# Masked attention and expert layers on one core: the last pattern matmul goes into the next head pair, transposes and maxima stand in twos, and the finishing work is spread

## The chip, the cores and the metric

The kernel runs on one core of a Trainium2 chip. The metric is the device time of the core in microseconds. Before the change it is 882.85 us, the median of three runs (878.72 to 883.02).

A core has engines that run side by side and each take their own instructions in order: PE (TensorE, matmuls and transposes), DVE (VectorE), ACT (ScalarE), POOL (GpSimd) and SP, which here mostly issues transfers (DMAs).

## The reference

Four batches with eight heads of 768 positions and 64 dimensions go through attention that lets a query see only the keys of its own hash bucket; the result, 3072 rows of 512, goes through a router and eight experts.

```python
q_bits = (einsum('bhsd,dk->bhsk', q, proj) > 0)      # 6 bits; the same for k
mask = q_bucket[:, :, :, None] == k_bucket[:, :, None, :]
scores = where(mask, (q @ k.T) / 8, -1e9)
attn = exp(scores - scores.max(-1)); attn /= attn.sum(-1) + 1e-9
x = (attn @ v).transpose(0, 2, 1, 3).reshape(3072, 512)
logits = x @ w_gate + modality_bias[modality_id]     # 8 experts
e = argmax(logits); gate = softmax(logits)[e]
out = gate * (relu(x @ w1[e]) @ w2[e])               # 512 -> 1024 -> 512
```

## The kernel before

**Two halves.** Up to some 540 us the core works on attention, in 16 steps, one for each pair of heads (`i` = 0 to 15, four to a batch). Behind that stands the expert phase, which multiplies blocks of 256 gathered rows (slots) with the weights of one expert, while the weights stream in as blocks of 512 KB (tile `raw`), are cast by ACT (L749) and split into a high and a low part by DVE or POOL (L751).

**A step and its letters.** In attention the scheduler orders every engine but PE; PE's order is written by hand. A step goes through six key tiles (`kt` = 0 to 5), and for each of them the table `PLAN` (L30 to L37) has a string. Each letter lets one generator go on by one piece:

- `S`, scores (L305, L306): one block of 128 keys by 512 queries for each head and then one for the last 256 queries of both. ACT exponentiates each (L318, L323), POOL adds the exponentials up (L326, tile `sp`).
- `A`, weighting (L341): the exponentials times the values, two key tiles later. `Q` (L359): column sums of the step before. `v`, `V` (L286): sums of the values.
- `M`, the maxima for the next step, i+1 (L239; L245 for two blocks of 256 at once). Each block goes into one of two buffers `psm`, from which DVE takes a maximum (L241, L247).
- `B`, late: the maxima, turned with a transpose into one of the buffers `psx` (L268), go into the operands on DVE (L270, L271).
- `W`, `T`, for steps i+3 and i+2: `W` splits the inputs (L162 on ACT, L166 on DVE and POOL). There are twelve `T`: six groups of four transposes (L180), copied out by ACT (L184), two sign blocks (L207; DVE, L209), and four pattern matmuls (L222): half 0 for both heads, then half 1 for both. Each pattern matmul fills a buffer `psx`, which L223 copies (ACT for half 0, DVE for half 1) and L224, a relu on ACT, reads too.

The buffers `psx` are two, shared by `T`, `B`, `V`, `Q` and the finishing; `psm` are two, the scores' `pss` two.

**Finishing.** When a batch's four steps are done, `finish` brings its sums into shape, takes reciprocals and routes its rows to experts (L374 to L413 and what they call), and `finish_x` turns six tiles of rows (L422), scales them on DVE (L424, tile `xs`, two buffers) and writes them to the memory tensor `x_d` (L426, on SP's queue). For batches 0 to 2 the letters `F`, `f` and `x` place this in steps 4 to 6, 8 to 10 and 12 to 14; for the last batch it runs among the first experts' work.

**The end.** Most slots are always done. Whether a few more are needed is known only on the chip: the tile `tot` holds two counts, and `conditional` (L904 on) makes two chains of branches from them, each of which loads its count into a register of every engine (L908, L910). With these inputs both chains are left at their first branch.

## Time and profile before

| quantity | value |
|---|---|
| median of three runs | 882.85 us |
| the profiled execution: its own time; span from first to last instruction | 881.03 us; 879.3 us |
| busy: PE, DVE, ACT, POOL | 814.8, 589.3, 502.9, 457.8 us |
| matmuls on PE | 5154 |
| granted TensorE clock, mean | 0.983 |
| step ends: sums matmuls L359 in the chain of waits | 81.00, 111.21, 141.47, 171.71 us |

The page has the busy time of each engine and its idle time by what ended it. The waits are a list for one engine: line and tile that waited, the engine and line that released it, and then the total, the number and the longest. Windows give busy times in stretches of the span. In the timeline a row is start, duration, engine, line, operation, tiles and shapes, and in brackets the idle time before it with its releaser; matmuls overlap, so from one to the next it is the starts that count, not the durations.

### The profile page before, as it was taken

What the parts mean: (1) busy time and instruction counts of PE and PEld (TensorE: products, weight loads), DVE (VectorE), ACT (ScalarE), POOL (GpSimd) and SP (SyncE); (2) the same over time, 40 slices, a digit from 0 to 9 for tenths busy, and PEclk for the clock granted to TensorE, in tenths of its full rate; (3) what the DMA queues carried; (4) which work ended last, traced back from release to release, by engine and by line L of the source; (5) the groups of instructions that cost most, each with busy time, mean ns of one, the idle gap of its engine ahead of it and who ended that gap; (6) DMA issues with size and microseconds to landing.
All of it is one profiled execution on the core that took longest, in us unless ns stands there. A gap on an engine that the chain in (4) does not pass through costs nothing.

```text
span 879.3 us, 14545 instructions
## 1 busy us (share of the span) xinstructions
PE 814.8 (93%) x5154; PEld 581.1 (66%) x5154; DVE 589.3 (67%) x1029; ACT 502.9 (57%) x949; POOL 457.8 (52%) x347
## 2 busy tenths in 40 slices
PE   6799999989899989899989998989999999999991
PEld 3555556555555555555555554879999999998981
DVE  6776766687676597676697685965656565657650
ACT  4466756656656656656655464455555555557550
POOL 5376687667877658868657697421222221212110
PEclk9699999999999999999999999999999999999996
DMA  6422213213323212322201432797777777679630
GB/s 170 109 73 73 66 43 91 63 28 91 88 75 91 73 28 81 88 82 66 54 18 38 143 110 81 198 251 243 223 222 234 221 213 227 218 225 300 204 129 14
DMA packets 76757, 110.92 MB, mean 126 GB/s; under 512 B 10495, under 2 KB 52095, under 8 KB 76672
## 3 DMA queue, kind: packets, MB, share of 16 engines
q1 hardware_dynamic: 71744, 96.72, 38.3%
q0 software_dynamic: 4928, 13.14, 4.0%
q8 instruction: 45, 0.74, 0.4%
q14 instruction: 40, 0.33, 0.1%
HBM read 84.83 MB, written 13.33 MB: 112 GB/s over the span
## 4 chain that ended last, share of the span: by engine, by line
PE 74%; DVE 12%; ACT 4%; DMA 3%; issue 3%; POOL 2%; SPq 0%; POOLq 0%; DVEq 0%; ACTq 0%
PE psu L341 13%; PE pss L305 8%; PE pss L306 6%; PE psm L239 5%; PE hps L786 5%; PE hps L788 4%; PE hps L787 4%; PE yps L830 4%; PE yps L828 4%; PE yps L829 4%; PE psx L180 3%; PE psx L207 2%; PE psm L245 2%; DVE mx L241 2%; DVE w L751 2%
## 5 line engine op out<-in xcount | busy, mean ns | idle before, releaser
L326 POOL TENSOR_TENSOR sp<-sp,pb 128x768 f32<-128x768 f32 x124 | 228.5, 1865 | 43.1 <-ACT pb L323 41.6
L751 DVE TENSOR_TENSOR w<-raw,w 128x1024 fp32r<-128x1024 f32 x108 | 136.7, 1268 | 90.6 <-ACT w L749 88.7
L749 ACT CAST w<-raw 128x1024 fp32r<-128x1024 f32 x112 | 117.0, 1047 | 61.5 <-PE yps L830 51.5
L241 DVE TENSOR_REDUCE mx<-psm 128x1 f32<-128x512 f32 x192 | 128.5, 686 | 26.3 <-PE psm L239 24.9
L341 PE MATMUL psu<-pb,vt 128*64 128x512 f32 (+1 forms) x768 | 144.8, 498 | 0.0
L318 ACT ACTIVATE pb<-pss 128x512 f32<-128x512 f32 x192 | 114.9, 599 | 48.8 <-PE pss L306 38.0
L323 ACT ACTIVATE pb<-pss 128x512 f32<-128x512 f32 x96 | 57.5, 599 | 132.8 <-PE pss L306 131.1
L786 PE MATMUL hps<-xh,w 128*128 128x256 f32 x384 | 108.9, 284 | 3.7 <-DVE hl L793 3.6
L787 PE MATMUL hps<-xl,w 128*128 128x256 f32 x384 | 108.9, 284 | 0.0
L788 PE MATMUL hps<-xh,w 128*128 128x256 f32 x384 | 108.5, 283 | 0.0
L341 PEld LDWEIGHTS psu<-pb,vt 128*64 128x64 f32 x768 | 46.7, 136 | 87.4 <-issue 87.2
L763 POOL DMA_INDIRECT xg<-x_d,tb x26 | 30.9, 1190 | 126.6 <-DMA tb<-tab 88.7
L836 POOL DMA_INDIRECT out<-y,tb x26 | 32.7, 1257 | 109.7 <-ACT y L835 56.2
L828 PE MATMUL yps<-w,hl 128*128 128x512 f32 x208 | 82.8, 398 | 0.8 <-DVE hl L816 0.8
L830 PE MATMUL yps<-w,hh 128*128 128x512 f32 x208 | 81.4, 391 | 0.0
L247 DVE TENSOR_REDUCE mx<-psm 128x2 f32<-128x512 f32 x96 | 66.1, 688 | 22.8 <-PE psm L245 17.8
L829 PE MATMUL yps<-w,hh 128*128 128x512 f32 x208 | 81.2, 390 | 0.0
L305 PE MATMUL pss<-m_0g,s_0g 128*128 128x512 f32 x192 | 77.9, 406 | 0.0
L166 POOL TENSOR_TENSOR n<-qk,n 128x384 fp32r<-128x384 f32 x36 | 40.5, 1130 | 70.9 <-ACT n L162 60.7
L786 PEld LDWEIGHTS hps<-xh,w 128*128 128x128 f32 x384 | 73.4, 192 | 5.1 <-DVE hl L793 4.3
L787 PEld LDWEIGHTS hps<-xl,w 128*128 128x128 f32 x384 | 73.6, 192 | 1.7 <-issue 1.2
L788 PEld LDWEIGHTS hps<-xh,w 128*128 128x128 f32 x384 | 73.5, 192 | 0.0
(210 smaller groups left out, 1766.7 us busy)
## 6 DMA issues: line engine op xcount, KB each, us to landing
raw<-moe_w SPq DMA_DIRECT2D x112, 512.0 KB
qk<-q SPq DMA_DIRECT2D x32, 192.0 KB
qk<-k SPq DMA_DIRECT2D x32, 192.0 KB
vt<-v SPq DMA_DIRECT2D x16, 384.0 KB
x_d<-xs SPq DMA_DIRECT2D x24, 256.0 KB
m_1g<-m_1g SPq DMA_DIRECT2D x16, 192.0 KB
s_1g<-s_1g SPq DMA_DIRECT2D x16, 192.0 KB
m_0g<-m_0g SPq DMA_DIRECT2D x15, 192.0 KB
```

The lines of the kernel that those rows point to most:

```text
L241: nc.vector.tensor_reduce(out=mx[:, qt + j, hi, 0:1], in_=mp, axis=AX.X, op=ALU.max)
L305: nc.tensor.matmul(out, t["s1"][h][:, ks], t["m1"][h][:, cs], start=True, stop=False)
L326: (nc.vector if h and i in CFG["spd"] else nc.gpsimd).tensor_tensor(out=t["sp"][:, h], in0=(t["pb"][0] if kt == 1 else t["sp"])[:, h], in1 ...
L341: nc.tensor.matmul(t["u"][part][64 * h:64 * h + 64, 0:w], t["v"][:, h, kt], t["pb"][kt][:, h, COLS[part]], start=False, stop=(kt == NT - 1 ...
L749: nc.scalar.copy(out=hi, in_=r)
L751: (nc.gpsimd if pool else nc.vector).tensor_tensor(out=lo, in0=r, in1=hi.bitcast(F32), op=ALU.subtract)
L786: nc.tensor.matmul(hps, lo[:, c, fs], xh[:, c], start=(c == 0), stop=False)
L787: nc.tensor.matmul(hps, hi[:, c, fs], xl[:, c], start=False, stop=False)
L788: nc.tensor.matmul(hps, hi[:, c, fs], xh[:, c], start=False, stop=(c == 3))
L828: nc.tensor.matmul(yps[g], hl[fc][:, gs], hi[:, fb], start=(fc == 0), stop=False)
L829: nc.tensor.matmul(yps[g], hh[fc][:, gs], lo[:, fb], start=False, stop=False)
L830: nc.tensor.matmul(yps[g], hh[fc][:, gs], hi[:, fb], start=False, stop=(fc == 7))
```

## The change

There are five parts in one edit.

1. The table. The last of a step's twelve `T`, the pattern matmul of head 1, half 1, gets a letter of its own, `P`, and is done in the next step behind its first score block. The groups of transposes stand two by two (`TT` in kt 0, 1 and 2), and so do most maxima (`MM`).
2. The finishing pieces have other places: new letters `e` and `E` let `finish` go on in the third and fourth step of a batch, and the six tiles of rows go into two steps, three each (`x` and `y`), instead of one.
3. In steps 0 and 1 two of the pattern copies (L223) each go from DVE to ACT; later steps are as before.
4. The last batch's six writes of rows are issued on ACT's queue instead of SP's.
5. `tot` has a third entry, worked out on DVE, that says whether any further slot is needed, and one branch on it stands around both chains.

```diff
 PLAN = (
-    "LvSMTMSASfMTMfx",
-    "SMTVMSASfMTMfx",
-    "SMTMSAQFlSMTMfx",
-    "SMSATFWSBfMx",
-    "SFWMSATSMfTFMWx",
-    "SMFTSATSTFWBx",
+    "LvSPMMTTSASfMMfexy",
+    "SMMTTSASfMVMey",
+    "SMMTTSAQFlSMMEfxy",
+    "SMSATWSBMEe",
+    "SWMSATFSMTMfWExe",
+    "SMTSATSBFfFfWe",
 )
...
-                (nc.vector.tensor_copy if half or i == 0 else nc.scalar.copy)(out=t["m1"][h][PT[h], hs], in_=pp[0:64, 0:HALF])
+                (nc.vector.tensor_copy if (half if i > 1 else i + h == 0) else nc.scalar.copy)(out=t["m1"][h][PT[h], hs], in_=pp[0:64, 0:HALF])
...
-            nc.sync.dma_start(out=xv[:, tt], in_=xs)
+            (nc.scalar if b == B - 1 else nc.sync).dma_start(out=xv[:, tt], in_=xs)
...
-            ts = chain(turn(i + 2), signs(i + 2), patterns(i + 2)) if i + 2 < NPR else iter(())
+            last, ts = ts, chain(turn(i + 2), signs(i + 2), patterns(i + 2)) if i + 2 < NPR else iter(())
...
+                    elif c == "P":
+                        next(last, None)
...
-                    elif c == "x":
-                        if i % 4 == 2:
-                            if kt == 0 and i > 4:
-                                xs = finish_x(i // 4 - 1, 0, NT)
-                            next(xs, None)
-                            next(xs, None)
-                            next(fins, None)
+                    elif c == "e" and i % 4 >= 2 or c == "E" and i == NPR - 2:
+                        next(fins, None)
+                    elif c == "x" and i % 4 == 2 or c == "y" and i % 4 == 3:
+                        if c == "x" and kt == 0 and i > 4:
+                            xs = finish_x(i // 4 - 1, 0, NT)
+                        next(xs, None)
+                        next(xs, None)
...
-        tot = const.tile([P, 2], I32, name="tot")
+        tot = const.tile([P, 3], I32, name="tot")
...
+        nc.vector.tensor_scalar(out=over[:, 0:1], in0=cu[:, E - 1:E], scalar1=SURE_BIG + 0.5, scalar2=None, op0=ALU.is_gt)
+        nc.vector.tensor_scalar(out=over[:, 1:2], in0=su[:, E - 1:E], scalar1=SURE_SML + 0.5, scalar2=None, op0=ALU.is_gt)
+        nc.vector.tensor_tensor(out=over[:, 0:1], in0=over[:, 0:1], in1=over[:, 1:2], op=ALU.max)
+        nc.vector.tensor_copy(out=tot[:, 2:3], in_=over[:, 0:1])
...
-        rest("b", SURE_BIG, NBIG, 0)
-        rest("s", SURE_SML, NSML, 1)
+        more = nc.values_load(tot[0:1, 2:3], min_val=0, max_val=1, skip_runtime_bounds_check_because="0 or 1")
+        with tc.If(more > 0):
+            rest("b", SURE_BIG, NBIG, 0)
+            rest("s", SURE_SML, NSML, 1)
```

On PE, where one ordinary step ends and the next begins (the numbers at names are buffers; L222 is a pattern matmul with its weight load, L268 `B`, L180 the transposes). Before:

```order
L222 MATMUL psx<-bits_172,pat 128x384
L305 MATMUL pss<-m_0g_111,s_0g_113 128x256
L306 MATMUL pss<-m_0g_115,s_0g_117 128x256
L305 MATMUL pss<-m_1g_112,s_1g_114 128x256
L306 MATMUL pss<-m_1g_116,s_1g_118 128x256
L222 LDWEIGHTS pat
L222 MATMUL psx<-bits_172,pat 128x384
L268 MATMUL psx<-identr,nm_1417 128x128 x2
L305 MATMUL pss<-m_0g_122,s_0g_124 128x512
L306 MATMUL pss<-m_0g_126,s_0g_128 128x512
L239 MATMUL psm<-s_0g_102,m_0g_100 128x512
L180 MATMUL psx<-identr,n_1340 128x128 x4
```

And at the same place with the change:

```order
L222 MATMUL psx<-bits_172,pat 128x384
L305 MATMUL pss<-m_0g_111,s_0g_113 128x256
L306 MATMUL pss<-m_0g_115,s_0g_117 128x256
L305 MATMUL pss<-m_1g_112,s_1g_114 128x256
L306 MATMUL pss<-m_1g_116,s_1g_118 128x256
L268 MATMUL psx<-identr,nm_1417 128x128 x2
L305 MATMUL pss<-m_0g_122,s_0g_124 128x512
L306 MATMUL pss<-m_0g_126,s_0g_128 128x512
L222 LDWEIGHTS pat
L222 MATMUL psx<-bits_172,pat 128x384
L239 MATMUL psm<-s_0g_102,m_0g_100 128x512 x2
L180 MATMUL psx<-identr,n_1340 128x128 x8
```

Between the last two pattern matmuls now stand `B` and a score block, the maxima are two at once, and the transposes eight at once.

Further on in the same step, from the end of kt 0 into kt 1, PE has with the change:

```order
L245 MATMUL psm<-s_0g_102,m_0g_100 128x256 x2
L239 MATMUL psm<-s_1g_103,m_1g_101 128x512
L305 MATMUL pss<-m_0g_122,s_0g_124 128x512
L306 MATMUL pss<-m_0g_126,s_0g_128 128x512
L239 MATMUL psm<-s_1g_103,m_1g_101 128x512
L245 MATMUL psm<-s_1g_103,m_1g_101 128x256 x2
L180 MATMUL psx<-identr,n_1340 128x128 x4
```

Before, four transposes stood between L245 and the first L239 and behind the second; now four blocks of maxima go by with one score block among them.

On DVE, from kt 2 into kt 3 of an ordinary step (L166 splits an input for step i+3, L364 adds the column sums, L255 joins maxima), the pieces stood before:

```order
L241 TENSOR_REDUCE mx_1157<-psm 128x1
L364 TENSOR_TENSOR gs<-gs,psx 128x384
L241 TENSOR_REDUCE mx_1157<-psm 128x1
L247 TENSOR_REDUCE mx_1157<-psm 128x2
L241 TENSOR_REDUCE mx_1157<-psm 128x1
L255 TENSOR_REDUCE m_1315<-mx_1157 128x8
L166 TENSOR_TENSOR n_1404<-qk,n_1404 128x6x64
```

With the change:

```order
L241 TENSOR_REDUCE mx_1157<-psm 128x1
L166 TENSOR_TENSOR n_1404<-qk,n_1404 128x6x64
L364 TENSOR_TENSOR gs<-gs,psx 128x384
L241 TENSOR_REDUCE mx_1157<-psm 128x1
L247 TENSOR_REDUCE mx_1157<-psm 128x2
L241 TENSOR_REDUCE mx_1157<-psm 128x1
L255 TENSOR_REDUCE m_1315<-mx_1157 128x8
```

The split L166 has come ahead of three maxima.

## Prediction

> **What bounds the kernel now.** The page comes first: PE is busy 93% of the span, no other engine above 67%, and three quarters of the chain that ended last is PE's.

> ```profile
> PE 814.8 (93%) x5154; PEld 581.1 (66%) x5154; DVE 589.3 (67%) x1029; ACT 502.9 (57%) x949; POOL 457.8 (52%) x347
> PE 74%; DVE 12%; ACT 4%; DMA 3%; issue 3%; POOL 2%; SPq 0%; POOLq 0%; DVEq 0%; ACTq 0%
> ```

> So time is to be won where PE stands still, and the list of PE's waits says for what (total, times, longest):

> ```profile
> PE psx L268 <- ACT s_0g L224: 16.1, 14, 2.0
> PE psm L239 <- DVE mx L247: 5.2, 6, 1.4
> PE hps L786 <- DVE hl L793: 3.6, 2, 3.0
> ```

> The largest comes once a step: `B` waits for a relu. The windows, one step each, show what a batch's finishing adds (columns: stretch, length, PE busy):

> ```profile
> 141.50:171.70 30.20, 29.12 (x186) 17.24 (x189) 19.91 (x35) 19.98 (x42) 22.22 (x16) 1.00 0.24 65
> 171.70:205.00 33.30, 31.09 (x202) 18.46 (x203) 28.68 (x59) 20.32 (x43) 21.70 (x16) 1.00 0.20 53
> 205.00:239.20 34.20, 31.78 (x214) 19.04 (x214) 23.97 (x43) 19.99 (x43) 29.34 (x23) 1.00 0.29 74
> 239.20:271.50 32.30, 31.07 (x202) 19.06 (x206) 23.25 (x39) 19.97 (x42) 22.08 (x16) 1.00 0.33 101
> ```

> The first is an ordinary step: PE idles 1.08. Finishing adds 1.97 + 2.66 + 1.95 = 6.6 of PE work, and idle time beyond 1.08 of 1.13 + 1.34 + .15 = 2.6.

> **The step's end**, a gain. The timeline of an ordinary step:

> ```profile
> 156.00 0.34 PE L222 MATMUL psx<-bits,pat 128*128 128x384 bf16 x1
> 156.04 0.41 PE L305 MATMUL pss<-m_0g,s_0g 128*128 128x256 f32 x1
> 156.30 0.28 PE L306 MATMUL pss<-m_0g,s_0g 128*128 128x256 f32 x1
> 156.41 0.28 PE L305 MATMUL pss<-m_1g,s_1g 128*128 128x256 f32 x1
> 156.65 0.34 PE L222 MATMUL psx<-bits,pat 128*128 128x384 bf16 x1
> 156.91 0.60 ACT L323 ACTIVATE pb<-pss 128x512 f32<-128x512 f32 x1 [0.34 <-PE pss L306]
> 157.53 0.49 ACT L224 ACTIVATE s_0g<-psx 64x384 fp32r<-64x384 f32 x1
> 158.07 0.36 PE L268 MATMUL psx<-identr,nm 128*128 128x128 f32 x2 [1.08 <-ACT s_0g L224]
> 158.27 0.47 PE L305 MATMUL pss<-m_0g,s_0g 128*128 128x512 f32 x1
> 158.58 0.40 PE L306 MATMUL pss<-m_0g,s_0g 128*128 128x512 f32 x1
> 158.81 0.40 PE L239 MATMUL psm<-s_0g,m_0g 128*128 128x512 f32 x1
> 159.05 0.46 PE L180 MATMUL psx<-identr,n 128*128 128x128 f32 x4
> 159.34 0.47 PE L239 MATMUL psm<-s_0g,m_0g 128*128 128x512 f32 x1
> ```

> The two pattern matmuls of 156.00 and 156.65 fill both `psx`; `B` needs one, and the first comes free when the relu at 157.53 is done. A pattern matmul holds PE's issue .04 (156.00 to 156.04), so PE stands from 156.69 to 158.07: 1.38. With the change `B` finds the buffer of an earlier pattern free and goes at 156.65, taking .20 (158.07 to 158.27), the score block .54 (to 158.81). `P` could go at 157.39 but needs the buffer of 156.00, free as before at 158.07, the exponential and relu ahead being the same: .68 remains. `P`'s own relu then stands behind the next exponential (.60 + .49), and the second of `TT`, which takes `P`'s buffer, waits for it; two maxima (.24 each, 158.81 to 159.05) and a transpose block (.29) cover all but .19. And what follows a pattern matmul comes late: 156.04 to 156.30 is .26, 156.30 to 156.41 .11; behind `B` that lay in the stall, behind `P` it costs .14. Together 1.38 − .68 − .19 − .14 = **.37 gained**.

> A matmul behind a transpose block takes .47 (159.34) instead of .40 (158.81): three blocks fewer stand alone, .2 gained.

> **The maxima**, a loss. How near may they stand?

> ```profile
> 152.31 0.39 PE L239 MATMUL psm<-s_1g,m_1g 128*128 128x512 f32 x1
> 152.74 1.29 DVE L241 TENSOR_REDUCE mx<-psm 128x1 f32<-128x512 f32 x2 [0.31 <-PE psm L239]
> 153.48 0.50 PE L245 MATMUL psm<-s_1g,m_1g 128*128 128x256 f32 x2
> 143.59 0.40 PE L305 MATMUL pss<-m_0g,s_0g 128*128 128x512 f32 x1
> 144.06 0.39 PE L239 MATMUL psm<-s_0g,m_0g 128*128 128x512 f32 x1
> ```

> With two `psm`, a third block must wait for the first one's reduction: at the earliest 1.17 behind the first block (152.31 to 153.48); a fourth for the second's, which ends at 154.03, 1.72 behind the first block and with a release of .04 1.76. A score block takes .47 (143.59 to 144.06). From kt 0 to kt 1 the changed order has two blocks, a score block, two blocks: the third comes at .24 + .24 + .47 = .95 and waits .22; the fourth would come at 1.41 and waits .35. From kt 1 to 2 a `V` stands between the first two; the third is then in time, the fourth waits about .3. From kt 2 to 3 three blocks in the first pattern: .22. Together **1.1 lost** a step. Less, if pieces of finishing stand there; more, if DVE brings its reductions late: L166 now stands ahead of three of them.

> ```profile
> L166 DVE TENSOR_TENSOR n<-qk,n 128x384 fp32r<-128x384 f32 x28 | 25.3, 905 | 15.5 <-issue 13.8 <-POOL sp L326 1.3
> ```

> By its mean of .9, where a score block and the sums give DVE room, I count nothing and .2 as the upper bound.

> So an ordinary step changes by −.37 − .2 + 1.1 = +.53, times 14: **+7.4**. Bounds: half of the maxima's waits covered, 14 × 0 = 0; .2 more each, +10.

> **Finishing.** Of the idle 2.6 a batch the spreading can take all, or (bound above) leave it and add as much again, since reciprocals and row scalings come on DVE ahead of reductions that PE now waits for. The pieces still are chains PE to DVE to PE, and I take 2.0 of idle time, counting in that `x` and `y` fill some waits of the maxima: −.6 for each of two batches. For the third, whose steps 14 and 15 are next, +.4. Sum **−.8**, from −8 to +8.

> **Steps 14 and 15.**

> ```profile
> 491.09 0.50 PE L239 MATMUL psm<-s_1g,m_1g 128*128 128x512 f32 x1 [1.39 <-DVE mx L247]
> 540.55 0.85 PE L359 MATMUL psx<-sp,ones 128*32 128x384 f32 x8 [0.68 <-POOL sp L326]
> ```

> The wait of 1.39 is for a reduction that DVE runs late in the crowded step 14; with three row tiles fewer it goes: −1.4. Three row tiles move to step 15, where PE waits for other engines anyway; −.7, as at 540.55. Against that, the rows land later, and in POOL's order a gather that needs them now stands ahead of three of the last step's `sp` additions, for which 540.55 waits: taken at +1.2, between 0 and two such additions, which the page has at 1.9 each (next fence). Sum **−.9**.

> ```profile
> L326 POOL TENSOR_TENSOR sp<-sp,pb 128x768 f32<-128x768 f32 x124 | 228.5, 1865 | 43.1 <-ACT pb L323 41.6
> ```

> **The last batch's rows.** In the chain and the timeline:

> ```profile
> 569.57 8.66 DMA x_d<-xs
> 578.33 1.29 DVE L424 TENSOR_TENSOR xs<-psx,rin 128x512 f32<-128x512 f32 x2 [5.18 <-DMA x_d<-xs]
> 579.53 3.48 DVE L751 TENSOR_TENSOR w<-raw,w 128x1024 fp32r<-128x1024 f32 x3
> 583.41 0.39 PE L786 MATMUL hps<-xh,w 128*128 128x256 f32 x1 [3.00 <-DVE hl L793]
> 853.21 2.90 DMA out<-y,tb
> 568.30 0.20 DVE L705 CAST tot<-lcu 128x1 int32<-128x1 f32 x1
> ```

> A row write, issued on SP's queue among the weight loads, takes 8.66; with both `xs` taken, DVE waits 5.18, its splits come late and PE loses 3.00. The nearest transfer on another queue, the output's, takes 2.90. By that DVE's wait falls away, and with it PE's: **−3.0**. ACT now stands at those issues until DVE has scaled the rows, its casts behind; bounds −3.0 and +1. The four operations for `tot` lie ahead of the same wait of DVE's and cost nothing; without that cover four times the .2 of the cast at 568.30, .8.

> [...]

> **One branch instead of two.**

> ```profile
> L908 POOLq TENSOR_LOAD <-tot x2: 306/404/503, 862.4 to 869.2; - x2
> L910 POOLq INC_SWDGE_SEM  x2: 1677/1692/1708, 867.5 to 870.4; - x2
> L970 POOLq DRAIN  x3: 40/107/6286, 872.1 to 879.0; - x3
> ```

> POOL ends the program: it loads the second count at 869.2, adds to its semaphore at 870.4 for 1.7, and then drains from 872.1 for 6.3. One chain fewer takes 872.1 − 869.2: **−2.9**. Bounds: 0, should the drain wait for the last output itself, and −6 if the drain shrinks too.

> **The copies in steps 0 and 1** are worth what DVE's being late and ACT's being late there differ by; such a piece takes some .5 (the relu at 157.53), two a step: 0, give or take 1.

> **Sum.** 7.4 − .8 − .9 − 3.0 − 2.9 = −.2 on the profiled 881.03: 880.8. The median stands 1.8 above that execution: **882.6**.

> **Rivals.** *The spreading fills the waits* (.30). Finishing's 6.6 of PE work a batch fall into what now idles behind the maxima: up to 4 × 1.1 = 4.4 a batch, of which I counted little, say 3 more on 2.5 batches (7.5), and 1.5 idle less on two batches (3): 882.6 − 10.5 = 872. For it: where PE waits for DVE only, any transposes cost nothing. Against: they need `psx` and DVE themselves.

> *DVE becomes the bound of the maxima* (.22). L166, the sums and finishing's chains run ahead of reductions; from a delay of .6, what a reduction takes, each goes on to PE in full. At .2 more in 14 steps (2.8) and two delays of .6 more in each of ten finishing steps (12, of which half falls into waits that are there: 6) it is 882.6 + 8.8 = 891, slower. For it: DVE is busy 28.68 of 33.30 in the first finishing step, 19.91 in an ordinary one. Against: the scheduler gives no more work, only another order.

> *The end gives nothing* (.08): rows land no sooner and the drain waits for the output: 882.6 + 5.9 = 888.5.

> **Numbers.** The forecast's own case keeps .40, with a range of its own from 877 to 888. Half a percent, 878.4 to 887.3, is about what a measurement of this kernel can tell from no change. All of the first rival (.30) lies below that, most of the second (.18 of .22) and half of the third above; of the own case I put .07 below, .27 within and .06 above. So faster .37, same .27 + .04 + .04 = .35, slower .06 + .18 + .04 = .28. The range goes from 869 to 893: with both large rivals in it, about .1 is left out on either side.

> **What would show it.** Right: `B`'s waits for L224 fall from 16.1 to little while L222 waits some .7 a step for the same; new waits of L239 and L245 for L241, L247 total about 15; ordinary steps take 30.7. In the experts 578.33's wait is short and 583.41's gone, and POOL has one TENSOR_LOAD at the end. Wrong: ordinary steps below 30.2 (maxima priced wrongly), finishing steps above 35 (the second rival), or a span that ends as late behind PE's last matmul as now.

## The result, and the profile after

The changed kernel takes 915.36 us (median of four runs, 911.22 to 917.89) against 881.25 us for the kernel before on the same chip (878.72 to 883.02). The ratio is 1.038, with a 95% interval from 1.036 to 1.041: **slower by 34 us**, outside the forecast's range of 869 to 893 (882.6 forecast).

The page and PE's list of waits of the kernel after:

```profile
PE 834.9 (91%) x5154; PEld 582.8 (64%) x5154; DVE 593.9 (65%) x1029; ACT 507.1 (55%) x953; POOL 453.1 (50%) x347
PE psm L239 <- DVE mx L241: 14.5, 9, 4.8
PE psx L222 <- ACT s_0g L224: 7.3, 13, 0.6
PE psx L180 <- ACT s_1g L224: 5.1, 13, 0.4
PE psx L422 <- DVE xs L424: 4.9, 1, 4.9
```

`B`'s wait of 16.1 us is gone, as it should be; `P` waits .6 and the second group of `TT` .4 in its place, each once a step. New are waits of 4.8 and 4.9 us. And PE is busy 20 us longer with the same 5154 matmuls: part of that is a slower clock (.92 in the third window below), and part is waiting, since the ends of matmuls are modelled and one that waits for its buffer also shows as longer (.50 instead of .39 below).

Windows of the kernel after: an ordinary step, and then two with most of the first batch's finishing (length, PE busy, ..., and, third from the end, the granted clock):

```profile
82.00:113.70 31.70, 30.39 (x184) 17.25 (x182) 20.11 (x36) 20.15 (x42) 21.98 (x16) 1.00 0.23 62
177.20:212.40 35.20, 33.04 (x212) 18.81 (x211) 26.51 (x51) 20.15 (x42) 22.25 (x16) 1.00 0.21 58
212.40:253.80 41.40, 33.96 (x200) 19.01 (x198) 26.75 (x51) 20.68 (x43) 23.95 (x18) 0.92 0.19 54
```

Before, these took 30.2, 33.3 and 34.2 us (by the marks below, which are the exact ones, 30.2, 34.4 and 33.1). The third has lost most, and in it the clock is down to .92.

The starts of the sums matmul L359, one a step, give the account. In us, before and after, from mark to mark:

| stretch | before | after | difference |
|---|---|---|---|
| up to the first mark | 80.93 | 81.99 | +1.06 |
| three ordinary steps | 90.71 | 95.24 | +4.53 |
| batch 0's finishing, four marks | 34.40, 33.08, 32.27, 30.23 | 35.15, 41.44, 34.04, 31.86 | +12.51 |
| batch 1's, four marks | 34.41, 33.78, 32.29, 30.21 | 35.14, 40.13, 33.55, 31.81 | +9.94 |
| batch 2's and the last steps | 34.16, 32.70, 25.40, 15.98 | 35.66, 29.81, 33.26, 15.70 | +6.19 |
| from the last mark to the end | 338.75 | 339.52 | +.8 |

Every ordinary step costs 1.51 us more. Fourteen times that is 21.1; beyond it stand 6.5 for batch 0, 3.9 for batch 1, 1.7 at the end of attention, 1.1 at its beginning and .8 in the experts. This account takes the ordinary loss for every step; with the order alone (below) a finishing step of batches 0 and 1 loses .4 to 1.5.

**The wait of 4.8 us and what follows it.** PE's timeline and windows, after:

```profile
214.45 0.40 PE L306 MATMUL pss<-m_0g,s_0g 128*128 128x512 f32 x1
219.65 0.79 PE L239 MATMUL psm<-s_0g,m_0g 128*128 128x512 f32 x1 [4.80 <-DVE mx L241]
220.67 0.63 PE L306 MATMUL pss<-m_1g,s_1g 128*128 128x512 f32 x1
219.65:226.00 6.35, 6.35 (x21) 2.38 (x22) 1.75 (x4) 1.11 (x2) 0.00 (x0) 0.50 0.00 0
```

A matmul that takes .40 before the wait takes .63 behind it: for 6.35 us the granted clock is .50, and then 1.00 again. The wait costs 4.8 and the slow clock half of 6.35, together 8.0 us; that is more than the 6.9 by which this step lost beyond an ordinary step's loss (8.36 − 1.51), so the rest of its finishing has become a little shorter. In batch 1 the same wait, 4.81 us, is followed by 3.42 us at half clock (362.57 to 365.99) and costs 6.5. What PE waited for is on DVE:

```profile
210.07 0.68 DVE L241 TENSOR_REDUCE mx<-psm 128x1 f32<-128x512 f32 x1
210.78 1.42 DVE L591 TENSOR_TENSOR l<-lg,bias 128x48 f32<-128x48 f32 x1
...
214.17 1.39 DVE L166 TENSOR_TENSOR n<-qk,n 128x384 fp32r<-128x384 f32 x1
215.48 0.19 DVE L614 TENSOR_REDUCE rsum<-rex 128x6 f32<-128x48 f32 x1
215.71 1.54 DVE L615 TENSOR_SCALAR rsum<-rsum 128x6 f32<-128x6 f32 x1
217.16 0.54 DVE L362 COPY gs<-psx 128x384 f32<-128x384 f32 x1
217.63 0.17 DVE L616 RECIPROCAL rec<-rsum 128x6 f32<-128x6 f32 x1
217.72 1.28 DVE L617 COPY rec<-ktok 128x6 int32<-128x6 int32 x1
218.92 0.68 DVE L241 TENSOR_REDUCE mx<-psm 128x1 f32<-128x512 f32 x1
```

Between two reductions DVE does the whole router chain, the sums and the split L166: 8.1 us. The scheduler set it there. In the kernel before the same lines (numbered two lower there) stand between reductions in small lots, and are shorter:

```profile
196.22 0.21 DVE L589 TENSOR_TENSOR l<-lg,bias 128x48 f32<-128x48 f32 x1
200.27 0.16 DVE L613 TENSOR_SCALAR rsum<-rsum 128x6 f32<-128x6 f32 x1
```

What makes them long is POOL. Two rows after, and one before:

```profile
208.52 3.62 POOL L326 TENSOR_TENSOR sp<-pb,pb 128x768 f32<-128x768 f32 x2
215.11 3.87 POOL L326 TENSOR_TENSOR sp<-sp,pb 128x768 f32<-128x768 f32 x2
200.94 1.01 POOL L166 TENSOR_TENSOR n<-qk,n 128x384 fp32r<-128x384 f32 x1 [6.46 <-ACT n L162]
```

After, POOL works from 207.55 to 218.98 with gaps of at most .1 us, and the long pieces end as a POOL instruction ends: L591 at 212.20 (POOL's addition at 212.14), L617 at 219.00 (218.98). Before, POOL stood idle for 6.46 us, and most of the chain fell into that pause. The ten router pieces (L591 to L604, L614 to L617) take 6.5 us after and 2.5 before; the 4.0 between is most of the wait of 4.8. Those among them that only reduce or take a reciprocal are not longer (.17 to .20).

**The ordinary step.** Its waits in PE's timeline, after:

```profile
129.45 0.40 PE L306 MATMUL pss<-m_0g,s_0g 128*128 128x512 f32 x1
130.38 0.32 PE L222 MATMUL psx<-bits,pat 128*128 128x384 bf16 x1 [0.54 <-ACT s_0g L224]
130.48 0.70 PE L239 MATMUL psm<-s_0g,m_0g 128*128 128x512 f32 x2
131.02 0.45 PE L180 MATMUL psx<-identr,n 128*128 128x128 f32 x4
131.87 0.53 PE L180 MATMUL psx<-identr,n 128*128 128x128 f32 x4 [0.40 <-ACT s_1g L224]
135.60 0.39 PE L306 MATMUL pss<-m_0g,s_0g 128*128 128x512 f32 x1
136.08 0.50 PE L239 MATMUL psm<-s_1g,m_1g 128*128 128x512 f32 x1
136.67 0.51 PE L245 MATMUL psm<-s_1g,m_1g 128*128 128x256 f32 x2
137.02 0.80 PE L180 MATMUL psx<-identr,n 128*128 128x128 f32 x8
```

And what the second transposes wait for, the relu behind `P`, on DVE and ACT:

```profile
130.74 0.55 DVE L223 CAST m_1g<-psx 64x384 fp32r<-64x384 f32 x1
131.33 0.48 ACT L224 ACTIVATE s_1g<-psx 64x384 fp32r<-64x384 f32 x1 [0.38 <-DVE m_1g L223]
```

By starts, with .24 for a matmul: `P` waits 130.38 − 129.69 = .69 (forecast .68); the second transposes 131.87 − 131.31 = .56 (forecast .19), since the relu waits .38 for DVE's copy out of the same buffer, which stands behind the three operations of `B`; the maxima at 136.08 wait .24 and at 136.67 .35 (forecast .22 and .35), and two more in the step .36 and .23. And a matmul that has waited holds the next one up: from 136.67 to 137.02 it is .35, where from 158.81 to 159.05 before, without a wait, it is .24. Three of the maxima's waits cost .11 each in this way, and the second transposes' .08: .4 a step beyond the waits themselves.

### The profile page after: what moved, and what is told of

Read it like the earlier page. It is cut to its first block, busy times and chain, and to the rows that moved or that the text cites. A ratio compares the mean times of both kernels' runs of the same rounds, so it can differ in the third digit from the quotient of the medians.

```text
span 914.3 us, 14521 instructions
## 1 busy us (share of the span) xinstructions
PE 834.9 (91%) x5154; PEld 582.8 (64%) x5154; DVE 593.9 (65%) x1029; ACT 507.1 (55%) x953; POOL 453.1 (50%) x347
## 4 chain that ended last, share of the span: by engine, by line
PE 71%; DVE 13%; ACT 5%; DMA 4%; issue 3%; POOL 1%; SPq 0%; POOLq 0%; DVEq 0%; ACTq 0%; another core or an unknown queue 0%
PE psu L341 13%; PE pss L305 7%; PE pss L306 6%; PE yps L835 5%; PE yps L837 4%; PE yps L836 4%; PE hps L795 4%; PE hps L794 4%; PE hps L793 4%; PE psm L239 4%; DVE mx L241 3%; PE psx L207 3%; PE psx L180 3%; PE psm L245 2%; PE psx L222 2%
## 5 line engine op out<-in xcount | busy, mean ns | idle before, releaser
L326 POOL TENSOR_TENSOR sp<-sp,pb 128x768 f32<-128x768 f32 x124 | 225.5, 1843 | 60.9 <-ACT pb L323 60.7
L758 DVE TENSOR_TENSOR w<-raw,w 128x1024 fp32r<-128x1024 f32 x108 | 142.1, 1317 | 94.3 <-ACT w L756 92.5
L341 PE MATMUL psu<-pb,vt 128*64 128x512 f32 (+1 forms) x768 | 147.4, 506 | 0.0
L241 DVE TENSOR_REDUCE mx<-psm 128x1 f32<-128x512 f32 x192 | 128.0, 685 | 21.1 <-PE psm L239 18.9
L323 ACT ACTIVATE pb<-pss 128x512 f32<-128x512 f32 x96 | 57.5, 599 | 127.6 <-PE pss L306 118.3
L793 PE MATMUL hps<-xh,w 128*128 128x256 f32 x384 | 108.9, 285 | 1.6 <-DVE hl L800 1.6
L247 DVE TENSOR_REDUCE mx<-psm 128x2 f32<-128x512 f32 x96 | 65.9, 686 | 31.3 <-PE psm L245 31.0
L166 POOL TENSOR_TENSOR n<-qk,n 128x384 fp32r<-128x384 f32 x36 | 37.0, 1034 | 94.6 <-ACT n L162 86.5
L305 PE MATMUL pss<-m_0g,s_0g 128*128 128x512 f32 x192 | 78.5, 409 | 0.5 <-issue 0.5
L793 PEld LDWEIGHTS hps<-xh,w 128*128 128x128 f32 x384 | 73.4, 191 | 3.2 <-DVE hl L800 2.4
```

The lines of the kernel that those rows point to most:

```text
L241: nc.vector.tensor_reduce(out=mx[:, qt + j, hi, 0:1], in_=mp, axis=AX.X, op=ALU.max)
L305: nc.tensor.matmul(out, t["s1"][h][:, ks], t["m1"][h][:, cs], start=True, stop=False)
L326: (nc.vector if h and i in CFG["spd"] else nc.gpsimd).tensor_tensor(out=t["sp"][:, h], in0=(t["pb"][0] if kt == 1 else t["sp"])[:, h], in1 ...
L341: nc.tensor.matmul(t["u"][part][64 * h:64 * h + 64, 0:w], t["v"][:, h, kt], t["pb"][kt][:, h, COLS[part]], start=False, stop=(kt == NT - 1 ...
L758: (nc.gpsimd if pool else nc.vector).tensor_tensor(out=lo, in0=r, in1=hi.bitcast(F32), op=ALU.subtract)
L793: nc.tensor.matmul(hps, lo[:, c, fs], xh[:, c], start=(c == 0), stop=False)
```

## The experiments

**The order alone, the finishing alone.** Two runs, each with one of the first two parts:

```diff
 # P, TT and MM; F, f and x where they were
-    "LvSMTMSASfMTMfx", "SMTVMSASfMTMfx", "SMTMSAQFlSMTMfx", ... "SMFTSATSTFWBx",
+    "LvSPMMTTSASfMMfx", "SMMTTSASfMVMfx", "SMMTTSAQFlSMMfx", ... "SMFTSATSFWBx",
```

> Part 1 alone: P, TT and MM in the table, all finishing pieces at the places they had before. Theory: the ordinary step's +1.5 us (31.7 instead of 30.2) is all the order's, so 14 steps cost about 21 us, the first marks come 1 us late, and the waits of 4.8 us that stand in the changed kernel's finishing steps are gone, since the router's pieces are back: 903 us. Rival: the maxima in twos alone put DVE's router pieces ahead of reductions, 4.8 us again in two steps: about 912 us.

```diff
 # F, f, e, E, x, y at the new places; S, M, T as before
+    "LvSMTMSASfMTMfexy", "SMTVMSASfMTMey", "SMTMSAQFlSMTMEfxy", "SMSATWSBMEe", "SWMSATFSMTMfWExe", "SMTSATSTFfFfWBe",
```

> Part 2 alone: finishing pieces at their new places, score blocks, maxima, transposes and patterns as before. Theory: the new places by themselves gather the router's pieces on DVE ahead of a maximum, so two waits of 3 to 5 us come in the second finishing step of batches 0 and 1, and the row tiles moved into the last step wait for DVE as in the changed kernel: 892 to 897 us, ordinary steps 30.2. Rival: only maxima in twos are hurt by a late DVE, and single ones hide it: 876 to 883 us.

Order alone: 896.92 us (one run; before 881.33), ordinary steps 31.7, the step that took 41.4 takes 34.5. Finishing alone: 888.11 (one run), ordinary steps 30.2, that step 33.65. The first theory holds for the ordinary steps and for the missing wait; the time is below its 903, since the finishing steps lose less than 1.5 us each. The second theory falls: neither part by itself brings the wait of 4.8 us (the longest for a maximum is .9 with the order alone, 2.0 with the finishing alone). It takes the new places and the maxima in twos together. What the order alone costs is 15.6 us, what the finishing alone 6.8; the whole change costs 34. The finishing alone leaves batches 0 and 1 about where they were (+.7 and −.1 us by the marks) and loses 6.3 us in the last four stretches, with a wait of 3.6 us for POOL's additions `sp` at the last sums (.7 before). The order's window that is to be compared with 212.40:253.80 above:

```profile
211.50:246.00 34.50, 32.25 (x206) 18.50 (x205) 23.92 (x44) 20.59 (x42) 28.56 (x22) 1.00 0.26 73
```

**Only the first half of the finishing put back.**

```diff
 # against the changed kernel: F and f at their old places, the rest stays
-    "SMMTTSASfMVMey", "SMSATWSBMEe", "SWMSATFSMTMfWExe", "SMTSATSBFfFfWe",
+    "SMMTTSASfMVMfey", "SMSATFWSBfMEe", "SFWMSATSMfTFMWExe", "SMFTSATSFWBe",
```

> The changed kernel with the first half of the finishing (the letters F and f) at its old places; P, TT, MM and the row tiles in two steps stay. Theory: in the changed kernel the router's chain on DVE (L591 to L617, with a split L166 among it) meets the maxima of kt 2 and 3, where PE then waits 4.8 us and runs at half clock behind it; at its old places the chain is over before: the second finishing steps fall from 41.4 and 40.1 us to 34.5 to 36 us, and the kernel takes 902 to 906 us, its steps 13 to 15 unchanged. Rival: the chain costs the maxima in twos the same wherever it stands in that step: 912 to 917 us.

892.91 us, 22 us less than the changed kernel. The window that answers to 212.40:253.80, and a little ahead of it, at the chain's old place, a row of DVE's and one of POOL's:

```profile
211.80:244.40 32.60, 31.54 (x200) 18.00 (x198) 23.38 (x43) 20.02 (x42) 27.48 (x21) 1.00 0.28 63
204.50 0.13 DVE L617 COPY rec<-ktok 128x6 int32<-128x6 int32 x1
207.12 1.02 POOL L166 TENSOR_TENSOR n<-qk,n 128x384 fp32r<-128x384 f32 x1 [8.06 <-ACT n L162]
```

The second finishing steps take 32.6 and 33.5 us instead of 41.4 and 40.1, at clock 1.00, even less than expected: 8.8 + 6.6 of the 22 us. That places the loss: it is the late `F` and `f`. The router pieces stand in a row here too (seven of them between two reductions), but in a pause of POOL's of 8.06 us, and the ten take 1.9 us. So standing in a row is not by itself what costs; in the changed kernel the row stands under POOL's additions and where maxima are due. How much each of the two is worth is not separated by a run. The theory had steps 13 to 15 unchanged, and there the stretch of 33.26 us fell to 25.97 as well, while the one ahead of it took 2.1 us more (31.86). So the late finishing had also spoiled the way from step 14 into step 15, by 5.2 us net, and the time came out below the theory's 902 to 906.

**The last batch of row tiles.** In the changed kernel step 15 has a wait of 4.88 us for a row tile, and ahead of it DVE shows a subtraction of 9.97 us, under POOL's additions:

```profile
533.57 14.37 POOL L326 TENSOR_TENSOR sp<-sp,pb 128x768 f32<-128x768 f32 x8
543.13 9.97 DVE L758 TENSOR_TENSOR w<-raw,w 128x1024 fp32r<-128x1024 f32 x1 [0.17 <-ACT w L756]
553.76 1.12 PE L422 MATMUL psx<-ident,ut 128*128 128x128 f32 x4 [4.88 <-DVE xs L424]
```

```diff
-                    elif c == "x" and i % 4 == 2 or c == "y" and i % 4 == 3:
+                    elif c == "x" and i % 4 == 2 or c == "y" and i % 4 == (2 if i == 14 else 3):
```

> The changed kernel with one thing put back: the third batch's six row tiles all in step 14 instead of three there and three in step 15. Theory: DVE's split of 9.97 us at 543 us, held off by POOL's unbroken additions, stays or not, but no row tile of step 15 waits behind it, so the wait of 4.88 us and the slow clock after it go: steps 13 to 15 together 6 to 8 us shorter, 907 to 909 us. Rival: the split simply holds up what comes next (the sums of v, the additions on DVE), and PE waits there instead: 913 to 916 us.

920.03 us (one run): above both ranges, with the mechanism of the rival. With all six row tiles in step 14 there are two other waits, 3.62 us for a `psx` that the sums on DVE hold, and in step 15

```profile
562.74 0.76 PE L336 MATMUL psu<-lone,vs 128*128 128x512 f32 x1 [4.78 <-DVE vs L293]
```

The row tile was only what happened to stand behind the late DVE. (In this run it is an addition L326 on DVE that takes 4.83 us.)

**How DVE and POOL stand to each other.** Three small kernels, whose output is zeros, run a DVE subtraction of two SBUF tiles of 128 by 1024 under a stream of POOL additions.

```diff
+ POOL: add; flag; add x n            DVE: wait for flag; subtract
```

> Not the model but two costs by themselves; the output is zeros, attention and experts are left out. First, a DVE subtraction of two SBUF tiles of 128 by 1024 that becomes ready while POOL runs 2, 4 or 8 additions without a pause: theory, it gets in only when POOL pauses, so it ends about 1.2 us behind the last addition (some 4, 8 and 15 us behind its own start); rival, it goes in turn with POOL's additions and takes 3 to 4 us however many follow. A reduction out of PSUM in the same place: about .7 us in either case. Second, PE in bursts of some 10 us with pauses of 1 to 4 us: theory, a pause of 4 us is always followed by several us at clock .5, one below 2 us never, and between them it depends on where the pause falls, so that the same pause gives both; rival, there is a fixed length from which on the clock falls.

> The two costs by themselves again (the output is zeros; attention and experts are left out), but POOL's additions now change between two tiles, as the kernel's do between two heads, so that one need not wait for the one before. In the first of these runs each addition built on the last, one started every 1.88 us for 1.80 us of work, and a DVE subtraction of two SBUF tiles took 2.73 us, getting its turn behind one addition. Theory: without that gap of .08 us POOL keeps the way, and DVE's subtraction ends only behind the last addition: about 4, 8 and 15 us for 2, 4 and 8 of them. Rival: turns are given all the same, 2.7 us each time. Pauses of PE: those of 1.9 us are not followed by a slow clock, those of 4 us and more always are, those of 2.6 and 3.3 us sometimes.

> The DVE subtraction of two SBUF tiles under a stream of six POOL additions by itself (the output is zeros; attention and experts are left out), 18 times, each time ready at another moment of the running addition (behind reductions of .1 to 1.2 us). In the changed kernel one such subtraction, ready .6 us into an addition, took 9.97 us, past five POOL instructions; in the two runs by themselves it was ready .13 us into one and took 2.73 us, past one. Theory: the moment decides, and from some point on, from the middle of an addition or late in it, the subtraction loses several turns and takes 4 to 10 us. Rival: turns are given at whatever moment, so that it takes 1.2 us plus what is left of the running addition, 1.3 to 2.8 us, and the 9.97 us has another cause.

In the first two it takes 2.73 us, whether 2, 4 or 8 additions follow, chained or not: the theory of a DVE that is locked out until POOL pauses falls. From the third, the first and the last of 18 rows, and the additions:

```profile
15.45 2.66 DVE L39 TENSOR_TENSOR lo<-raw,hi 128x1024 f32<-128x1024 f32 x1
...
247.41 1.68 DVE L39 TENSOR_TENSOR lo<-raw,hi 128x1024 f32<-128x1024 f32 x1
L45 POOL TENSOR_TENSOR sp<-sp,pb x128: 1793/1796/2780, 9.4 to 256.2; 128x768 f32<-128x768 f32 x128
```

Ready .23 us into an addition of 1.80 it takes 2.66, ready 1.20 into one 1.68, and evenly in between: what is left of the running addition, and 1.09 beyond its end; an addition behind it takes up to 2.78 instead of 1.80. A reduction out of PSUM in the same place took .68 in the second run, as L241 does above. Every one of the 18 ends 1.08 us behind the addition that it found running. The subtraction of 9.97 us ends 1.08 us behind a POOL instruction as well (553.10; the addition of 550.22 ends at 552.02), but behind the fifth. Why it let four go by is thereby **not explained**; none of the 18 moments does it. It stays open.

**Pauses of PE and the clock.** The same first two kernels run PE in bursts of 34 us and more with pauses between them. In the traces the clock changes only at moments that lie a whole number of 3.41 us apart within a run (in the first at 256.68, 301.05, 502.44 and so on; in the changed kernel at 226.04, 362.58, 365.98, 553.72 and 557.14, with 40, 1, 55 and 1 times 3.41 between them), so each pause can be laid on a grid of stretches of 3.41 us. The table has the pauses (length as the profile has it in brackets), what follows them, and how long PE was idle in one grid stretch: where the slow clock followed, the stretch that had just ended, and where it did not, the one with most of the pause:

| pause, us | times | followed by clock .5 | idle in a stretch, not followed | idle in a stretch, followed |
|---|---|---|---|---|
| 1.51 and .79 | 11 | 0 | up to 1.51 | |
| 2.24 | 10 | 2 | 1.1 to 1.96 | 2.18, 2.24 |
| 2.96 | 8 | 6 | 1.51, 1.96 | 2.02 to 2.96 |
| 3.69 | 6 | 4 | 1.90, 1.96 | 2.21 to 2.71 |
| 4.42 | 1 | 1 | | 3.27 |

Two pauses of 2.96 us, the first without a slow clock (first run), the second with one (second run); each time the stretch with most of the pause, and the next one:

```profile
417.11:420.52 3.41, 1.45 (x4) 0.38 (x2) 1.86 (x3) 0.00 (x0) 1.00 0.00 0
420.52:423.93 3.41, 2.41 (x6) 1.22 (x7) 0.91 (x2) 0.00 (x0) 1.00 0.01 2
172.18:175.59 3.41, 1.39 (x3) 0.68 (x4) 1.90 (x3) 0.00 (x0) 1.00 0.00 0
175.59:179.00 3.41, 3.41 (x6) 1.32 (x5) 0.00 (x0) 0.00 (x0) 0.50 0.00 0
```

In these two runs no length of pause divides the cases: those of 2.24, 2.96 and 3.69 us came with and without a slow clock behind them, according to where they fell, as the first run's theory had it. In all 13 cases that are followed, PE was idle for 2.02 us or more of the stretch that had just ended (3.41 − 1.39 above); in the 23 others for 1.96 at most (3.41 − 1.45). Two of the six pauses of 3.69 us passed, divided between two stretches, with 1.90 and 1.96 in the fuller one; the one of 4.42 had 3.27 in one stretch. In the model the two kinds are less well divided: the wait of 3.00 us before has 1.85 of it in one stretch and passes, the 2.72 of the copies' run has 2.02 and does not, but in the first 45 us stretches with 1.73, 1.74 and 1.90 of idle time before and with 1.67 and 1.68 after are followed by clock .5 too, and one with 2.65 before (2.00 to 5.41) is not. In the two small kernels the slow stretch lasts 3.41 us (10 times) or 6.83 (3 times), and begins between 1.4 us before and 1.4 us behind the pause's end.

**`P` alone.**

```diff
-    "LvSMTMSASfMTMfx", ... "SMFTSATSTFWBx",
+    "LvSPMTMSASfMTMfx", ... "SMFTSATSFWBx",
```

> Only the last pattern matmul moves into the next step; transposes and maxima stay apart. Theory: the stall at the step's end falls from 1.38 us to about .7 plus .1, and since transposes stand apart the next one does not wait for P's buffer: ordinary steps 29.7 to 29.9, 14 steps save 5 to 7 us: 874 to 877 us. Rival: P's relu, one exponential later, makes the next transposes wait what was saved: 880 to 883 us.

880.14 us, beside 881.33 for before: the time is the rival's, the steps are the theory's. Ordinary steps take 29.68, .55 less; attention ends 4.1 us sooner. But in the second finishing steps a wait of 2.00 us for a row tile is followed by the slow clock (.50 from 232 to 234 us; 35.4 instead of 33.1), and in the experts the wait that was 3.00 us before is now

```profile
579.97 0.58 PE L788 MATMUL hps<-xh,w 128*128 128x256 f32 x1 [3.88 <-DVE hl L795]
579.97:585.70 5.73, 5.73 (x27) 5.73 (x28) 3.40 (x5) 1.51 (x3) 4.51 (x5) 0.51 0.94 304
```

with 5.73 us at half clock behind it, where before none followed.

**The three small parts, one by one.** The copies in steps 0 and 1 (part 3 of the change, against before):

> Part 3 alone: two pattern copies each of steps 0 and 1 on ACT. Theory: they cost about nothing, the first sums stay at 80.9 us: 880 to 882 us. Rival: the first sums' 1.06 us delay in the changed kernel is theirs: 882 us with the first sums at 82.0 us.

885.47 us (one run): the first mark comes .8 later. The four kernels with these copies have it at 81.66 to 84.59, the other seven at 79.77 to 81.36, so most of the changed kernel's delay there is theirs. Of the rest much is the experts' wait of 3.00 us again: here it is 2.72, but half clock follows, until 591 us (.50 in all windows from 584 to 590).

The last batch's rows on ACT's queue (part 4):

> Part 4 alone: the last batch's row writes on ACT's queue. The changed kernel's experts took as long as before although its end is 1.75 us shorter. Theory: the rows land sooner and DVE's wait of 5.18 us goes, but ACT stands at the issues with its casts behind it, and gathers of rows come later, so PE waits in other places for about what it no longer waits in one: within 2 us of before. Rival (the prediction's): PE's 3.00 us go and nothing comes in their place: 3 us faster.

881.51 us; the ratio to before is 1.002, from 1.000 to 1.003: nothing. It is the theory in its outcome but not in its reason:

```profile
576.67 1.51 DVE L424 TENSOR_TENSOR xs<-psx,rin 128x512 f32<-128x512 f32 x2 [5.02 <-DMA x_d<-xs]
```

DVE waits 5.02 for the landing where it waited 5.18. On a queue of its own, beside the weight stream, the row write won DVE .16 us, and PE's wait in the experts is 3.5 us instead of 3.00. In the changed kernel it did land sooner (7.00 us in the chain instead of 8.66; DVE waited 2.4), and there gathers came later instead, with waits of 2.59 and 1.11 us.

One branch at the end instead of two (part 5):

> Part 5 alone: one branch at the end instead of two. Theory: PE's last matmul comes as before, and the span ends about 1.8 us sooner behind it, as in the changed kernel (15.9 instead of 17.7 us). Rival (the prediction's): 2.9 us sooner. Second rival: the drain waits for the last output and nothing is won.

879.45 us; the ratio is .999, from .997 to 1.001. At the end the branch does more than forecast. POOL's first load of a count and its last drain:

```profile
L922 POOLq TENSOR_LOAD <-tot x1: 499/499/499, 864.8 to 864.8; - x1
L977 POOLq DRAIN  x3: 40/107/6286, 870.6 to 877.5; - x3
```

From load to drain it is 5.8 us, where before it was 862.4 to 872.1, 9.7: 3.9 saved. PE's last matmul starts 14.0 us ahead of the end instead of 18.0 (863.69 and 861.24; the 15.9 and 17.7 of the expectation were read from a product ahead of the last). In the middle of the experts a gather's wait of 2.35 us and a slow clock behind it (.50 from 592 to 594 us) took most of that back.

**A version that is faster.** `P`, the single branch, and the row tiles of batches 0 to 2 one key tile later, behind the sums of `v`:

```diff
+    "LvSPMTMSASfMTMf", "SMTVMSASfMTMfx", "SMTMSAQFlSMTMfx", "SMSATFWSBfMx", "SFWMSATSMfTFMWx", "SMFTSATSFWBxx",
-                            if kt == 0 and i > 4:
+                            if kt == 1 and i > 4:
```

> The kernel before with P alone, the single branch at the end, and the row tiles x one key tile later, behind the sums of v, which in the run with P alone waited 2.01 us in the second finishing steps and were followed by a slow clock. Theory: ordinary steps 29.7 us as with P alone, the second finishing steps 33 us or below instead of 35.4, the end 1.8 us shorter: 872 to 876 us, .5 to 1% faster. Rival: the row tiles' wait for DVE comes back at their new place: 877 to 881 us.

872.75 us against 881.98 on the same chip; the ratio is .989, from .987 to .991: 1.1% faster than the kernel before. Its windows:

```profile
80.90:110.60 29.70, 29.15 (x188) 17.23 (x188) 20.00 (x35) 20.08 (x42) 22.28 (x16) 1.00 0.24 68
203.70:235.90 32.20, 30.87 (x200) 18.02 (x198) 23.94 (x42) 20.19 (x42) 27.94 (x21) 1.00 0.25 52
```

## Why the prediction was wrong

It forecast no change, +34 came; by its own terms:

- **Finishing, −.8: this step failed.** It was sized by today's idle time of 2.6 us a batch, bounded at +8 for the whole, and added to the maxima's loss as if the two were independent. Alone it was not far off: +.7 and −.1 us for batches 0 and 1. Together with the maxima in twos the two batches take 7.7 and 6.2 us longer than with the order alone, through one wait of 4.8 us in each. I had seen L166 come ahead of three maxima and listed that row of DVE's order, and looked no further along the finishing steps, where the whole router chain stood between two reductions, drawn out from 2.5 to 6.5 us under POOL's additions. The second rival, DVE as the bound of the maxima, was the right mechanism; its price was wrong in shape, small delays in ten steps instead of one of 8.0 and one of 6.5 us.
- **The clock was in no term.** The wait of 4.80 us cost 8.0, since 6.35 us at half clock followed. Before, the longest wait behind the start-up, 3.00 us, was followed by full clock, and I took a wait's price to be its length.
- **The ordinary step, +.53: the right sign, a third of the size.** 1.51 was measured. `P`'s wait and the maxima's waits were priced nearly right (.69 for .68; 1.2 for 1.1). Missed were the second transposes, which waited .56 instead of .19 because the relu waits for DVE's copy (+.37), and what waiting matmuls cost beyond their waits (+.4). Together with .53, the maxima's .1, and .1 that two blocks of eight transposes take beyond twice a block of four (137.02 to 137.66 is .64, not .58) these give 1.5. `P` alone gains .55, the forecast's .37 without the .19 for the paired transposes; the twos take away 31.7 − 29.7 = 2.0.
- **Steps 14 and 15, −.9:** they lost 5.0 (32.70 + 25.40 before, 29.81 + 33.26 after). With `F` and `f` back 5.2 went away, so it is the late finishing that spoils them, by a DVE that is late; how it comes to be as late as the 9.97 us row shows is open. POOL's additions, priced here at +1.2, held PE up for 3.6 us with the finishing alone and for .7 in the changed kernel.
- **Row writes, −3.0:** wrong. Alone on ACT's queue they left DVE's wait at 5.02 us for 5.18, and the time at 1.002 of before. The 2.90 I went by was of a transfer at a time without a weight stream. Why DVE waited only 2.4 in the changed kernel is not shown.
- **One branch, −2.9:** right, 3.8 to 3.9 at the end. The experts as a whole still took .8 longer than before, with waits of 2.59 and 1.11 for gathered rows and slow clock behind them (.61 in the mean from 628.4 to 632.8).
- **The first copies, 0 give or take 1:** +.8, in its bounds.

Of the signs that would show it wrong, "finishing steps above 35 (the second rival)" is what came. One of the signs of being right, new waits for the maxima of about 15 us in all, came too, 14.5 in the list, but by luck: 9.6 of it are the two long waits.

## What to carry to other kernels

In this kernel two buffers go round between the maxima's matmul and its reduction. With the maxima in twos PE waited 1.2 us a step for them, and the 8.1 us that the scheduler had put on DVE between two reductions became a wait of 4.8 on PE. So read the reducing engine's order along every special step, not along the ordinary one alone, and beside it what POOL does at that time: DVE's pieces of .2 us took up to 1.5 under its additions. Price a wait of PE by what follows it as well: of the 24 pauses of 2.24 to 3.69 us in the two small kernels 12 were followed by half clock, for 3.41 or 6.83 us, according to where they fell, and the changed kernel's three of 4.80 to 4.88 us all were. Before packing pieces together try the one move that removes a wait: `P` alone, with its neighbours left apart, gained .55 us a step, and the packing around it lost 2.0.
